# Reading the first block's queries in fp32 on a hardware queue, constants on the other queue, and a new instruction order, in a fused attention and feed-forward kernel

## The chip, the core and the metric

The kernel runs on one core of a Trainium2 chip. A core has TensorE (PE: matmuls and their weight loads), VectorE (DVE), ScalarE (ACT), GpSimd (POOL) and SyncE (SP), each with its own instruction stream that is worked off in order, and 16 DMA engines that all queues share. SP and ACT issue DMAs on hardware queues; GpSimd issues on the software queue, the only one here that converts fp32 to fp16 on the way. The metric is the device time of one execution in microseconds. A profile is of one execution; its span is the time from the first to the last instruction of the program.

## The reference

Attention over 4 batches, 8 heads, 768 positions and head size 64, with a sliding window of 128 and 4 sink positions that all see, and then a feed-forward layer on the 3072 tokens of 512.

```python
scores = scale * np.matmul(q, k.transpose(0, 1, 3, 2))
keep = is_sink | in_window              # j < 4, or 0 <= i - j < 128
a = softmax(np.where(keep, scores, -1e9))
x = np.matmul(a, v)                     # heads side by side: 3072 x 512
h = x @ w_in                            # 512 x 2048
g = h * (1.0 / (1.0 + np.exp(-1.702 * h)))
return g @ w_out                        # 2048 x 512
```

All inputs and the output are fp32. The kernel computes in fp16 with fp32 sums.

## The kernel before

**Tiling.** The sequence is cut into 24 blocks of 128 positions, 6 to a batch. A block holds all 8 heads. `ORDER` gives the places in which they are worked on: the first four places are blocks 0, 6, 12 and 18, the first of each batch, which need no block before them; then 1, 2, 3 and so on. Two neighbouring places make a pair, and the feed-forward layer runs over 12 pairs (`g`, numbered from 0) of 256 tokens.

**A block's steps.** Queries and keys (`qkn`) are transposed to `qkT`: on TensorE for the first eight places (`tq`, lines 398 and 405) with an eviction by VectorE or ScalarE (lines 355 and 359), by a DMA of SP for later pairs (line 433). Scores go to `own` and, for blocks with one before them, `prv` and `snk` (lines 481 and 510). For the first four places two matmuls per block write the causal mask into `own` ahead of the scores (`masks`, line 473). VectorE packs, takes the maximum (`mx`, line 537) and subtracts it (`e`, line 578); ScalarE takes the exponent (`a`, line 617). `a` is transposed to `at`, on TensorE for the first six places (`ta`) and by a DMA of SP for the rest (line 682). GpSimd cuts `at` into two triangles, `at` and `atp` (the selects, lines 620 and 624). TensorE multiplies with the values (`av`, lines 709 to 719), VectorE norms (`xn`, lines 726 and 727), and `xn` is transposed to `xT`, on TensorE for early blocks (`tx`) and by a DMA of SP from pair 3 on (line 758).

**Feed-forward.** For a pair, 8 groups of `hT` (line 780) are followed by the gate on ScalarE (line 810; for pair 0 a tanh on ScalarE and a multiplication on VectorE, lines 794 and 801), and 4 steps for each of two outputs `o` (line 834), an eviction to `osb` and a store. `w_in` and `w_out` are each loaded in four pieces (`i0` to `i3` and `o0` to `o3`; lines 293 and 302).

**Loads.** The software queue of GpSimd loads and converts `q`, `k` and `v` of nearly all blocks, one DMA each (lines 277 and 284; `v` at line 255, after VectorE has set the ones column of `v65`, line 232). Blocks of the first four places are read in rows of eight positions (`big`), so a packet has 2 KB of fp32; later ones and all of `v` have packets of one head's row of 64. One load is different: the keys of place 0, named in `CFG["hw"]`, are read in fp32 by SP to `raw_k` (line 263) and rounded by VectorE to `qkn` (line 271). The constants `consts` (identity, mask) are also read by SP (line 226). `vsb`, the sinks' values, is zeroed once (line 231).

**Order.** Every step is added to a planner with the engines that it may run on and estimated costs, and the order of all 834 steps, with the engine of each, is written out in the string `SEQUENCE`, which `Plan.run` reads: `12t` is step 12 on GpSimd, and p, a, d, s stand for PE, ACT, DVE, SP. The costs (`xfer`, `post` and the others) were used where the order was searched; at run time only `SEQUENCE` counts. Since each load is a step, an edit to the list `loads` renumbers the steps.

Of the kernel before, what the change touches and what calls it, by code (L numbers as in the profile page):

```python
# [36 lines left out]
    gbatch={},  # L37
    tanh=(0, 1),
    last=(256, 128, 128),
    hw=["k0"],  # L40
    big=(0, 1, 2, 3),
    avb={0: ("mi", "mm"), 1: ("mi", "mm"), 2: ("mi", "mm")},
    hb={},
    tqb={0: ("mm", "mi"), 1: ("mm", "mi")},
    actq=0,
    after0=25.0,
    vsb=15.0,
    slack={'v': 1, 's': 1, 'x': 1, 'e': 0.0, 'p': 0.0},
    steady=8,
    after=8.0,  # L50
    loads="q0 q1 k1 q2 k2 q3 k3 v0 v1 i0 i1 v2 v3 i2 i3 o0 o1 q4 k4 v4 o2 q5 k5 v5 o3".split(),
)
RING = dict(qkn=4, qkt=4, qk0=2, e32=4, a16=4, at=4, atp=4, xn=2, xt=4, gt=3, osb=4, mm=3, own=1, pv=1, mi=1, th=2)

SEQUENCE = """
0s 10d 4d 37s 12t 7d 14t 11a 16t 13t 106p 38d 15t 9d 2d 103p 6d 23t 3d 101p 104a 20t 126p 102a 18t 107p 127d 17t
124p 19t 108d 149p 109d 125a 22t 147p 150a 110d 129p 25t 148a 130p 111d 112a 105t 131d 113a 114p 132d 170p 115a 26t
116p 133d 171a 118p 152p 21t 117a 119d 153p 135a 134d 29t 120p 8d 137p 136a 121d 172p 33t 138a 154d 122p 173a 30t  # L60
139p 156d 123a 175p 155d 174t 140a 141p 481p 142d 158a 24t 157d 143p 176p 482a 144d 160p 34t 159a 483d 145p 161a 27t
177d 162p 484p 163a 146d 28t 179d 166p 487p 485a 167d 181a 486d 493p 488a 178d 489d 490p 40t 494a 180d 39t 478p 491a
495d 182a 32t 492d 183p 164p 479a 165d 499p 36t 184a 480d 185p 42t 500a 187p 195p 186d 193p 501d 48t 189p 196a 496p
190d 194a 168p 188d 497a 217p 215p 197p 169a 498d 218a 198p 191p 43t 199d 514p 192a 508p 216d 515a 200d 518p 46t
201d 509p 519a 31t 202d 239p 502p 240a 52t 203d 219p 128t 237p 221d 503p 238a 204a 520p 67t 222d 220p 510p 5d 223d
93s 504p 225d 224d 1s 242p 49t 94s 511p 151d 226a 45t 505p 512d 241p 521a 51t 506d 516p 243d 54t 524p 517a 244d 205p
525a 528p 206d 253p 245d 529a 255p 207t 522p 254d 247d 256a 246d 530p 35t 523a 227p 97t 208p 248a 228d 258p 257p
209d 270s 531p 259d 210t 230p 532p 260d 231a 229t 211p 261d 526p 249s 232t 212d 533p 527a 263d 262d 44t 233p 60t
536p 234d 264a 55t 213p 534d 537p 214d 41t 271p 538p 50t 273d 265s 235p 250t 539p 236a 274d 272p 548p 540a 296s 275d
550p 276d 57t 549a 552p 58t 277d 283p 53t 553a 544p 285d 551a 266t 554p 545a 286d 284p 251p 555a 287d 542p 61t 252d  # L70
546p 47t 288d 267p 56t 547a 556p 543a 268d 564p 289d 557a 269s 278a 558p 541s 297p 559p 299d 290a 565p 279s 300d
298p 566p 535s 301d 560p 96s 302d 291s 567p 303d 309p 304a 280t 95s 561p 311d 568a 305s 310p 578p 562d 570p 312d
579a 322s 292t 576p 98d 281p 571a 572p 66t 282d 584p 306t 313d 573a 507s 577a 513s 293p 585a 580p 294d 64t 574p 314d
581a 295s 84t 592p 575a 315d 316a 63t 307p 593p 59t 308d 586p 73t 317s 582p 72t 594p 99t 583a 587p 70t 323p 604p
325d 348s 595p 605a 326d 588p 596a 318t 324p 600p 327d 328d 589p 601a 598p 329d 65t 590d 335p 591s 78t 608p 563s
337d 62t 612p 609a 338d 69t 599a 336p 602p 613a 68t 339d 319p 603a 341d 340d 82t 606p 76t 620p 320d 607a 85t 342a
614p 100d 321s 79t 610p 361p 75t 330a 621p 343s 363d 91t 615p 611a 364d 331s 362p 616p 365d 622p 367d 366d 617p 623p
618a 632p 374s 624d 638p 636p 344t 639a 349p 637a 630p 351d 350p 626p 631a 352d 332t 345p 627a 634p 633a 346d 628p
353d 81t 640p 354d 629a 635a 333p 368a 648p 334d 642p 355d 347s 375p 356a 643p 569s 377d 641a 376p 357s 649p 378d
644p 369s 379d 650p 380d 645p 625s 656p 619s 646d 597s 381d 387p 358t 657a 400s 662p 389d 668p 663a 370t 651p 669a  # L80
359p 652a 388p 654p 360d 77t 658p 390d 74t 660p 659a 391d 80t 655a 371p 393d 392d 661a 71t 664p 372d 676p 665a 382a
373s 401p 670p 403d 647s 402p 671p 404d 394a 383s 666p 405d 677p 667a 406d 395s 672p 407d 413p 408a 673p 415d 384t
684p 674d 678p 416d 685a 409s 414p 679p 90t 417d 426s 692p 87t 680d 385p 418d 693a 396t 696p 419d 386d 686p 682p 88t
687a 397p 410t 683a 690p 697a 398d 688p 691a 399s 698p 689a 420a 694p 411p 699p 412d 695a 421s 700p 427p 675s 710p
429d 452s 712p 711a 430d 428p 701p 713a 422t 431d 720p 432d 724p 721a 702d 439p 725a 86t 433d 718p 441d 92t 716p
719a 442d 83t 440p 714p 717a 89t 423p 715a 732p 434a 424d 704p 443d 425s 445d 733p 444d 435s 722p 446a 705p 723a
681s 465p 447s 706p 467d 734p 703s 468d 466p 750p 436t 469d 735p 751a 470d 707p 736a 448t 742p 708a 746p 743a 437p
747a 738p 438d 748p 471d 739a 449p 749a 740p 472a 450d 744p 451s 453p 726p 745a 473s 455d 727p 456d 737s 454p 728p
741a 653s 457d 760p 459d 458d 752p 474t 729p 753a 460a 761p 730d 772p 762p 773a 461s 766p 763p 767a 780p 764a 770p
475p 462t 771a 768p 781a 476d 776p 769a 778p 777a 788p 779a 463p 774p 464d 782p 775a 477s 789p 765s 783p 731s 784p  # L90
790p 785p 796p 786d 791p 797a 754p 792a 808p 793s 709s 794p 787s 809a 802p 795a 755p 803a 806p 756p 807a 798p 800p
799a 757p 801a 804p 758d 822p 759s 805a 810p 816p 811p 823p 812p 824p 813p 817p 814a 825p 818p 826a 815s 828p 819p
827s 829p 820d 830p 831p 821s 832a 833a
"""


# [69 lines left out]
def kernel(  # L166
# [28 lines left out]
    plan = Plan(RING)  # L195
# [26 lines left out]
    def by(e):  # L222
        return nc.sync if e == SP else nc.scalar
# [19 lines left out]
    )  # L243

    def sw(key, cost, fn, xfer, **kw):
        return plan.add(POOL, key, cost, fn, xfer=xfer, post=0.9, **kw)

    ld, qkn = {}, {}

    def load_block(which, b, key, after=0.0):  # L250
        bb, r = divmod(b, 6)
        pair, i = divmod(PLACE[b], 2)
        src = {"q": q, "k": k, "v": v}[which][bb, :, r * P : (r + 1) * P, :].rearrange("h s d -> s h d")
        if which == "v":
            return sw(key, 0.88, lambda b=b, x=2: nc.gpsimd.dma_start(v65[:, b, :, 0:D], src), 0.88 if pair < 4 else 0.95, deps=[z_1], after=after)  # L255
        w = "qk".index(which)
        buf = qkn[pair]
        if which + str(PLACE[b]) in CFG["hw"]:
            raw = const.tile([P, H * D], FP32, name=f"raw_{which}{b}")
            n = CFG["hw"].index(which + str(PLACE[b]))  # L260
            src = {"q": q, "k": k}[which][bb, :, r * P : (r + 1) * P, :].rearrange("h (t e) d -> t h (e d)", e=8)
            got = plan.add(
                {SP: 0.45, ACT: 0.6}, -120 + n, 0, lambda e, src=src, raw=raw, x=9: by(e).dma_start(raw, src), xfer=0.75, post=0.6
            )

            def round16(e, b=b, w=w, i=i):
                dst, src = buf()[:, i, w].rearrange("p h d -> p (h d)"), raw
                if e == ACT:
                    nc.scalar.copy(out=dst, in_=src)
                else:  # L270
                    (nc.vector if e == DVE else nc.gpsimd).tensor_copy(out=dst, in_=src)

            return plan.add({DVE: 0.42, ACT: 0.6, POOL: 0.8}, -110 + n, 0, round16, deps=[got], take=[buf])
        if PLACE[b] in CFG["big"]:
            return sw(
                key, 0.64,
                lambda b=b, w=w, i=i: nc.gpsimd.dma_start(  # L277
                    buf()[:, i, w].rearrange("p h d -> p (h d)"),
                    {"q": q, "k": k}["qk"[w]][bb, :, r * P : (r + 1) * P, :].rearrange("h (t e) d -> t h (e d)", e=8),
                ),  # L280
                0.7, take=[buf], after=after,
            )
        return sw(
            key, 0.88, lambda b=b, w=w, i=i: nc.gpsimd.dma_start(buf()[:, i, w], src), 0.88 if pair < 4 else 0.95,  # L284
            take=[buf], after=after,
        )
# [4 lines left out]
    def load_w_in(f, key):  # L291
        def go(f=f, x=0):
            nc.gpsimd.dma_start(  # L293
                w_in16[:, :, bass.ts(f, 512)],
                moe_w_in.rearrange("(c p) f -> p c f", p=P)[:, :, bass.ts(f, 512)],
            )

        return sw(key, 0.8, go, 2.5)

    def load_w_out(f, key):  # L300
        def go(f=f, x=1):
            nc.gpsimd.dma_start(
                w_out16[:, bass.ts(f, 4)],
                moe_w_out[bass.ts(f, 512), :].rearrange("(c p) f -> p c f", p=P),
            )

        return sw(key, 0.8, go, 2.5)

    for n, what in enumerate(CFG["loads"]):
        w, x = what[0], int(what[1:])  # L310
# [584 lines left out]
```

## Time and profile before

| | before |
|---|---|
| times | 229.1, 229.35, 229.35 us; median 229.35 |
| profiled execution | 228.31 us, span 226.6 us |
| TensorE busy | 214.5 us (95%) |
| VectorE, ScalarE, GpSimd busy | 136.2, 136.6, 113.5 us |
| DMA moved | 32.47 MB, mean 143 GB/s |
| granted TensorE clock | 1.00 |

The page cuts the span into 40 slices of 5.7 us; each digit is the busy share in tenths:

```profile
PE   1889899999999999999899999999999999999994
DVE  0899898998896852796286677843957371111010
DMA  6999999999999999999998998999998072042112
```

TensorE starts after the first loads and is nearly always busy from the second slice to the last. The DMA engines are busy from the first slices on until three quarters of the span. A chain or a wait that names a DMA tells which load or transpose landed last before an instruction could start.

### The profile page before, as it was taken

What the parts mean: (1) busy time and instruction counts of PE and PEld (TensorE: products, weight loads), DVE (VectorE), ACT (ScalarE), POOL (GpSimd) and SP (SyncE); (2) the same over time, 40 slices, a digit from 0 to 9 for tenths busy, and PEclk for the clock granted to TensorE, in tenths of its full rate; (3) what the DMA queues carried; (4) which work ended last, traced back from release to release, by engine and by line L of the source; (5) the groups of instructions that cost most, each with busy time, mean ns of one, the idle gap of its engine ahead of it and who ended that gap; (6) DMA issues with size and microseconds to landing.
All of it is one profiled execution on the core that took longest, in us unless ns stands there. A gap on an engine that the chain in (4) does not pass through costs nothing.

```text
span 226.6 us, 5625 instructions
## 1 busy us (share of the span) xinstructions
PE 214.5 (95%) x2378; PEld 151.7 (67%) x2378; DVE 136.2 (60%) x243; ACT 136.6 (60%) x190; POOL 113.5 (50%) x135
## 2 busy tenths in 40 slices
PE   1889899999999999999899999999999999999994
PEld 0658876776784785675675685686765956856763
DVE  0899898998896852796286677843957371111010
ACT  2588696796746766367349249848585669613511
POOL 8955654698980689397071670780816112300000
PEclk9999999999999999999999999999999999999999
DMA  6999999999999999999998998999998072042112
GB/s 128 174 205 196 178 191 191 156 142 137 134 164 157 203 210 156 120 219 134 148 174 133 260 138 144 127 147 130 150 116 198 4 191 38 17 138 77 66 46 93
DMA packets 123512, 32.47 MB, mean 143 GB/s; under 512 B 114880, under 2 KB 120416, under 8 KB 123488
## 3 DMA queue, kind: packets, MB, share of 16 engines
q0 software_dynamic: 71792, 13.51, 79.6%
q1 hardware_dynamic: 51552, 18.55, 44.7%
q8 instruction: 18, 0.29, 0.6%
q10 hardware_dynamic: 144, 0.07, 0.1%
q14 instruction: 6, 0.05, 0.1%
HBM read 27.46 MB, written 6.29 MB: 149 GB/s over the span
## 4 chain that ended last, share of the span: by engine, by line
PE 77%; DMA 10%; POOL 5%; DVE 2%; ACT 1%; SPq 1%; issue 1%; POOLq 0%; DVEq 0%
PE o L834 33%; PE hT L780 31%; DMA w_in<-in_moe_w_in_dram 6%; DMA at<-a 4%; PE own L481 3%; PE av L715 2%; PE av L719 2%; PE av L709 2%; PE prv L481 2%; POOL qkn L277 2%; SPq L682 1%; POOL v L255 1%; POOL w_in L293 1%; PE tq L405 1%; PE snk L510 1%
## 5 line engine op out<-in xcount | busy, mean ns | idle before, releaser
L780 PE MATMUL hT<-xT,w_in 128*128 128x256 f16 (+1 forms) x896 | 94.1, 257 | 1.4 <-DMA xT<-xn 0.6
L834 PE MATMUL o<-w_out,gT 128*128 128x512 f16 (+2 forms) x416 | 91.8, 363 | 0.0
L810 ACT ACTIVATE gT<-hT 128x512 f16<-128x512 f32 x88 | 50.9, 597 | 58.7 <-PE hT L780 58.4
L780 PEld LDWEIGHTS <-w_in 128*128 128x128 f16 x896 | 75.3, 98 | 14.5 <-DMA xT<-xn 1.1
L834 PEld LDWEIGHTS <-gT 128*128 128x128 f16 x416 | 37.2, 98 | 32.2
L620 POOL TENSOR_SCALAR_AFFINE_SELECT atp<-at 128x1024 f16<-128x1024 f16 (+1 forms) x22 | 22.2, 1009 | 65.7 <-DMA at<-a 64.7
L527 DVE COPY_PREDICATED own<-consts,prv 128x1024 f32<-128x1024 uint16 x20 | 24.6, 1229 | 24.3 <-PE prv L481 24.2
L537 DVE TENSOR_REDUCE mx<-own 128x8 f32<-128x1024 f32 (+1 forms) x28 | 29.7, 1068 | 0.9 <-PE own L481 0.4
L578 DVE TENSOR_TENSOR e<-own,mx 128x1024 f32<-128x1024 f32 (+1 forms) x28 | 29.8, 1066 | 0.9
L617 ACT ACTIVATE a<-e 128x1056 f16<-128x1056 f32 (+1 forms) x28 | 26.2, 952 | 4.9 <-issue 2.6
L624 POOL TENSOR_SCALAR_AFFINE_SELECT at<-at 128x1024 f16<-128x1024 f16 (+1 forms) x22 | 22.5, 1024 | 1.5
L355 DVE COPY osb<-o 128x512 f32<-128x512 f32 (+1 forms) x12 | 8.0, 666 | 24.3 <-PE o L834 24.3
L284 POOL DMA_DIRECT2D qkn<-in_k_dram x20 | 17.8, 902 | 7.4 <-DMA w_out<-in_moe_w_out_dram 5.1
L255 POOL DMA_DIRECT2D v<-in_v_dram x24 | 21.4, 902 | 0.0
L726 DVE RECIPROCAL rcp<-av 128x8 f32<-128x8 f32 (+1 forms) x28 | 5.5, 195 | 26.5 <-PE av L719 26.4
L284 POOL DMA_DIRECT2D qkn<-in_q_dram x20 | 17.8, 894 | 2.3 <-DMA qkn<-in_k_dram 0.7
L810 ACT ACT_TABLE_LOAD x14 | 18.0, 1283 | 0.2
L727 DVE TENSOR_TENSOR xn<-av,rcp 128x512 f16<-128x512 f32 (+1 forms) x28 | 17.2, 615 | 1.0
L715 PE MATMUL av<-v,at 128*128 128x65 f16 x192 | 17.0, 194 | 0.6 <-POOL at L624 0.5
L617 ACT ACT_TABLE_LOAD x13 | 16.7, 1283 | 0.2
L715 PEld LDWEIGHTS <-at 128*128 128x128 f16 x192 | 14.2, 98 | 2.5 <-POOL at L624 1.2
L481 PEld LDWEIGHTS <-qkT 64*128 64x128 f16 x352 | 10.2, 96 | 7.8 <-issue 5.1
(56 smaller groups left out, 165.9 us busy)
## 6 DMA issues: line engine op xcount, KB each, us to landing
out_dram<-osb SPq DMA_DIRECT2D x23, 256.0 KB, 2.5
qkn<-in_q_dram POOLq DMA_DIRECT2D x24, 128.0 KB, 5.3
v<-in_v_dram POOLq DMA_DIRECT2D x24, 128.0 KB, 5.6
qkn<-in_k_dram POOLq DMA_DIRECT2D x23, 128.0 KB, 8.6
w_in<-in_moe_w_in_dram POOLq DMA_DIRECT2D x4, 512.0 KB, 10.2
w_out<-in_moe_w_out_dram POOLq DMA_DIRECT2D x4, 512.0 KB, 11.6
at<-a SPq DMA_TRANSPOSE x18, 3.3
raw_k<-in_k_dram SPq DMA_DIRECT2D x1, 256.0 KB, 4.6
```

What stands on the lines that cost most here:

```text
L255: return sw(key, 0.88, lambda b=b, x=2: nc.gpsimd.dma_start(v65[:, b, :, 0:D], src), 0.88 if pair < 4 else 0.95, deps=[z_1], after=after)
L284: key, 0.88, lambda b=b, w=w, i=i: nc.gpsimd.dma_start(buf()[:, i, w], src), 0.88 if pair < 4 else 0.95,
L527: nc.vector.copy_predicated(out=own(lo, hi).rearrange("p l j s -> p (l j) s"), mask=later.unsqueeze(1).to_broadcast((P, 4 * (hi - lo), P)) ...
L537: lambda lo=lo, hi=hi, own=half, small=small: nc.vector.tensor_reduce(out=small[:, lo:hi], in_=own(lo, hi), axis=AX.X, op=ALU.max),
L578: nc.vector.tensor_tensor(out=e32()[:, 512 * lo : 512 * hi].rearrange("p (l j s) -> p l j s", j=4, s=P), in0=own(lo, hi), in1=small[:, lo: ...
L617: nc.scalar.activation(out=a16()[:, lo:hi], in_=e32()[:, lo:hi], func=AF.Exp, scale=scale)
L620: nc.gpsimd.affine_select(out=atp()[:, lo : lo + n], in_=at()[:, lo : lo + n], pattern=[[0, n], [-1, P]], compare_op=ALU.is_gt, fill=0.0, ...
L624: nc.gpsimd.affine_select(out=at()[:, lo : lo + n], in_=at()[:, lo : lo + n], pattern=[[0, n], [1, P]], compare_op=ALU.is_ge, fill=0.0, ba ...
L715: nc.tensor.matmul(acc[:, j], at()[:, c], v65[:, b, h], start=(r == 0), stop=(r == 0))
L780: nc.tensor.matmul(ht()[:, n], w_in16[:, c, bass.ts(f, P)], xt[g]()[:, tok, c], start=(c == 0), stop=(c == 3))
L810: lambda fs=fs, cols=cols, gt=gt, ht=ht: nc.scalar.activation(out=gt()[:, fs[0] : fs[-1] + 1, cols], in_=ht(), func=AF.Gelu_apprx_sigmoid),
L834: nc.tensor.matmul(po(), gt()[:, F, bass.ts(t, P)], w_out16[:, F, cols], start=(F == 0), stop=(F == NF - 1))
```

## The change

The queries of place 0 join its keys in `CFG["hw"]`: both are read in fp32 by SP, keys first, and rounded by VectorE. The constants may now be issued by SP or ACT, and the new order has them on ACT, ahead of its first table load. `q0` leaves the list of software loads. Some estimated costs are edited, and `SEQUENCE` is another one throughout.

```diff
-    hw=["k0"],
+    hw=['k0', 'q0'],
...
-    actq=0,
+    actq=1,
...
-    loads="q0 q1 k1 q2 k2 q3 k3 v0 v1 i0 i1 v2 v3 i2 i3 o0 o1 q4 k4 v4 o2 q5 k5 v5 o3".split(),
+    loads="q1 k1 q2 k2 q3 k3 v0 v1 i0 i1 v2 v3 i2 i3 o0 o1 q4 k4 v4 o2 q5 k5 v5 o3".split(),
...
-0s 10d 4d 37s 12t 7d 14t 11a 16t 13t 106p 38d 15t 9d 2d 103p 6d 23t 3d 101p 104a 20t 126p 102a 18t 107p 127d 17t
+0a 38s 8d 36s 2d 10d 4d 7d 18t 11a 12t 13t 39d 17t 104p 16t 37d 105a 19t 102p 15t 107p 103d 14t 6d 108p 21t 125p 24t
...
-        return plan.add(POOL, key, cost, fn, xfer=xfer, post=0.9, **kw)
+        return plan.add(POOL, key, cost, fn, xfer=xfer, **{"post": 1.1, **kw})
...
-                {SP: 0.45, ACT: 0.6}, -120 + n, 0, lambda e, src=src, raw=raw, x=9: by(e).dma_start(raw, src), xfer=0.75, post=0.6
+                {SP: 0.45, ACT: 0.6}, -120 + n, 0, lambda e, src=src, raw=raw, x=9: by(e).dma_start(raw, src), xfer=0.9, post=0.6
...
-                key, 0.64,
+                key, 0.56,
...
-        return sw(key, 0.8, go, 2.5)
+        return sw(key, 0.8, go, 2.5, post=2.0)
```

What the new order does with the steps that the prediction speaks of, by the instruction order of both programs:

| | before | after |
|---|---|---|
| SP, first | consts, raw_k | raw_k, raw_q |
| GpSimd, first loads (by block) | q0 k6 k12 q6 q12 v12 v6 k18 q18 v0, then i1 i2 | v0 q6 k6 k18 q18 v6 k12 q12, then i1 i2 i3 |
| then | sink keys, i3 i0 q1 q2 k1, sink keys, v18 k2 o0 o1 k3 q3 o2 o3 | sink keys, i0 v12 q2 k1 q1, zeroing of vsb, v18 k2 k3 o0, sink keys, q3 o1 o2 o3 |
| TensorE, first | masks, tq of block 0's keys and queries, tq of block 6's keys, scores of block 0 | tq of block 0's keys and queries, masks, scores of block 0, tq of block 6 |
| GpSimd, loads between the selects of places 11 and 13 (counted from 0) | v13 q19 v11 q15 v14 k20 k17 k21 k19 q17 k23 | v19 v11 |
| zeroing of vsb | VectorE | GpSimd |
| eviction of block 18's queries and of block 0's first `ta` | ScalarE | VectorE |
| eviction of `xT` of block 6 | VectorE | ScalarE |

More of the change, by code (lines that the diff above doesn't have):

```diff
@@ L57 @@
 SEQUENCE = """
-0s 10d 4d 37s 12t 7d 14t 11a 16t 13t 106p 38d 15t 9d 2d 103p 6d 23t 3d 101p 104a 20t 126p 102a 18t 107p 127d 17t
[L59 to L92, printed above, removed]
@@ L93 @@
-827s 829p 820d 830p 831p 821s 832a 833a
+0a 38s 8d 36s 2d 10d 4d 7d 18t 11a 12t 13t 39d 17t 104p 16t 37d 105a 19t 102p 15t 107p 103d 14t 6d 108p 21t 125p 24t
+109d 127p 126a 111d 25t 128a 110d 113a 171p 129t 112d 130p 115p 9d 20t 131p 114a 172d 150p 132d 22t 151a 148p 116d
+32t 134d 117p 149a 119p 133d 118a 153p 29t 136a 135d 121p 154p 28t 120d 173p 137a 138p 122d 174a 3t 156d 139a 123p
+140p 124a 155d 176p 142p 141a 157d 482p 23t 158d 144p 483a 485p 33t 145d 159a 143d 177p 486a 484d 161p 487d 162a
@@ new lines @@
+146p 160a 179d 488p 41t 147a 178d 163p 489a 181d 494p 164a 180d 495a 490d 491p 26t 182a 496d 106t 167p 165p 492a
+479p 168d 183a 40t 493d 184p 480a 166d 500p 27t 185a 481d 31t 186p 501a 188p 194p 187d 196p 35t 502d 190p 195a 497p
+191d 197a 61t 169p 189d 498a 218p 44t 216p 198p 170a 499d 219a 43t 192p 200d 515p 217a 193a 519p 201d 516a 50t 199p
+503p 202d 42t 204d 520a 203d 509p 240p 221p 220p 241d 30t 238p 222d 510p 239a 205a 504p 223d 521p 46t 224d 511p 226d
+5d 225d 94s 243p 505p 1s 227a 242p 49t 512p 522a 47t 506p 513d 34t 244d 517p 507a 175t 529p 245d 518a 64t 254p 530a
@@ new lines @@
+256p 246d 525p 52t 255a 248d 531p 257d 45t 526a 247d 206p 228p 207a 98t 259p 532p 229d 249a 271s 208t 209p 258p 210d
+231p 260d 533p 211t 523p 261d 230t 212p 524a 250s 232d 534p 262d 233t 213d 527p 263d 53t 234p 528a 537p 55t 264d
+235d 265a 538p 56t 535d 236p 70t 272p 539p 58t 274d 237a 266s 214p 251t 273p 540p 215a 275d 549p 541a 276d 297s 553p
+277d 550a 57t 543p 62t 278d 284p 51t 554a 547p 286d 48t 551p 548a 287d 267t 252p 552a 545p 544a 253d 285p 555p 546a
+288d 59t 268p 289d 556a 557p 279a 269d 559p 290d 270s 298p 565p 291a 300d 280s 560p 558a 301d 566p 95s 299p 567p
@@ new lines @@
+514s 302d 542s 304d 579p 303d 96s 568p 292s 580a 281t 305a 310p 571p 323s 312d 561p 152d 569a 311p 282p 313d 572a
+306s 293t 581p 314d 562p 283d 582a 577p 563d 54t 508s 99d 583p 67t 316d 315d 573p 584a 68t 294p 100d 574a 307t 575p
+578a 295d 593p 576a 296s 317a 585p 73t 308p 74t 587p 309d 65t 586a 318s 594p 69t 595p 60t 324p 596p 77t 326d 325p
+71t 605p 597a 327d 599p 606a 328d 588p 319t 600a 329d 613p 349s 336p 614a 81t 603p 338d 63t 607p 604a 330d 339d 320p
+608a 601p 321d 589p 602a 322s 611p 570s 609p 612a 536s 337p 598s 590p 610a 340d 331a 342d 621p 341d 615p 362p 343a
@@ new lines @@
+616p 364d 622p 344s 365d 617p 332s 591d 363p 623p 366d 618p 367d 629p 619a 345t 350p 620s 630a 564s 624p 352d 97s
+637p 333t 375s 368d 353d 346p 638a 639p 625a 347d 351p 76t 627p 640a 354d 90t 334p 355d 628a 631p 79t 356d 335d 641p
+82t 632a 348s 635p 80t 642a 633p 66t 636a 376p 72t 634a 643p 369a 378d 78t 649p 379d 644p 357a 377p 650p 380d 382d
+645p 381d 358s 659p 383a 370s 646p 660a 651p 647d 401s 388p 669p 390d 359t 389p 663p 670a 391d 652p 648s 664a 392d
+661p 85t 393d 655p 371t 662a 653d 360p 656a 394d 654s 665p 361d 592s 384s 657p 372p 658a 667p 666a 373d 395a 671p
@@ new lines @@
+374s 402p 672p 404d 385t 668a 396s 677p 405d 403p 673p 406d 83t 697p 407d 86t 678p 698a 408d 414p 75t 409a 674p 416d
+93t 685p 397t 417d 679p 686a 410s 675d 386p 101d 683p 427s 387d 415p 680p 684a 691p 681d 398p 692a 411t 689p 399d
+695p 418d 690a 400s 687p 419d 92t 696a 412p 89t 688a 420d 693p 413d 88t 699p 694a 84t 421a 428p 91t 700p 430d 717p
+431d 725p 422s 718a 429p 701p 432d 434d 702p 433d 453s 713p 703d 440p 714a 719p 442d 423t 441p 721p 720a 443d 726a
+715p 722a 87t 444d 711p 446d 445d 424p 712a 705p 716a 425d 435a 723p 426s 466p 733p 704s 468d 447a 436s 706p 469d
@@ new lines @@
+724a 734p 448s 467p 735p 470d 472d 626s 707p 682s 749p 437t 736p 750a 708p 737a 449t 753p 709a 743p 754a 739p 744a
+438p 740a 747p 439d 745p 471d 450p 746a 751p 748a 451d 727p 452s 741p 676s 454p 742a 728p 752a 456d 473a 455p 729p
+457d 761p 458d 730p 459d 474s 762p 460d 773p 731d 461a 763p 774a 462s 779p 475t 764p 732s 780a 710s 767p 765d 769p
+768a 463t 476p 770a 775p 477d 781p 771p 782a 776a 464p 772a 755p 465d 777p 478s 756p 778a 766s 789p 757p 790p 758p
+795p 759a 791p 796a 783p 797p 792p 798a 784p 793a 809p 794s 738s 785p 810a 799p 786p 800a 801p 787d 807p 788s 802a
@@ L94 @@
+803p 808a 805p 804a 823p 806a 811p 824p 812p 825p 813p 814p 817p 815a 818p 826p 816s 819p 827d 760s 820p 828s 829p
+821d 830p 831p 822s 832p 833a 834a
 """
@@ L305, in go @@
             )
-        return sw(key, 0.8, go, 2.5)
+        return sw(key, 0.8, go, 2.5, post=2.0)
     for n, what in enumerate(CFG["loads"]):
```

## Prediction

> **What bounds the kernel now.** I read the page first, then TensorE's waits, then the timeline of the first 14 us, then the table by stretches of time, and last the DMA issues with their landings.
>
> ```profile
> span 226.6 us, 5625 instructions
> PE 214.5 (95%) x2378; PEld 151.7 (67%) x2378; DVE 136.2 (60%) x243; ACT 136.6 (60%) x190; POOL 113.5 (50%) x135
> ```
>
> TensorE is busy for 214.5 of 226.6 us. The matmuls of the changed program are the same ones, so only the 12.1 us of idle time can move: 8.9 us before the last matmul ends at 223.5, and a tail of 3.1. TensorE's waits say where the 8.9 lies:
>
> ```profile
> PE own L473 <- DMA consts<-cconst: 2.9, 1, 2.9
> PE tq L398 <- DVE qkn L271: 2.4, 1, 2.4
> PE hT L780 <- DMA xT<-xn: 0.6, 1, 0.6
> PE hT L780 <- DMA w_in<-in_moe_w_in_dram: 0.6, 1, 0.6
> PE tx L745 <- DVE xn L727: 0.5, 2, 0.3
> PE av L715 <- POOL at L624: 0.5, 1, 0.5
> ```
>
> The first two are the start (5.26 us). Sorted by time, the gaps from 7.36 to 25.8 us add 2.27, and those from 60 to 119 us add 1.38 (0.15 at 60.9, 0.63 at 109.0, 0.53 at 115.1, 0.07 at 119.1). Between and after these TensorE never stops. The start in the timeline:
>
> ```profile
> 0.81 0.35 SPq L226 DMA_DIRECT2D consts<-cconst  x1
> 1.22 0.75 SPq L263 DMA_DIRECT2D raw_k<-in_k_dram  x1
> 1.32 0.68 POOL L277 DMA_DIRECT2D qkn<-in_q_dram  x1 [0.80 <-POOLq L876]
> 2.86 1.03 PE L473 MATMUL own<-consts 128*128 128x512 bf16 x2 [2.86 <-DMA consts<-cconst]
> 5.81 0.43 DVE L271 CAST qkn<-raw_k 128x512 f16<-128x512 f32 x1 [3.94 <-DMA raw_k<-in_k_dram]
> 6.29 1.07 PE L398 MATMUL tq<-consts,qkn 128*64 128x64 f16 x32 [2.40 <-DVE qkn L271]
> 8.18 0.61 PE L481 MATMUL own<-qkT 64*128 64x128 f16 x8
> 8.28 0.69 DVE L355 CAST qkT<-tq 128x512 f16<-128x512 f32 x1 [0.73 <-PE tq L398]
> 8.89 1.28 DVE L537 TENSOR_REDUCE mx<-own 128x4 f32<-128x512 f32 x2
> ```
>
> The mask matmuls (L473) fill dead time. What ends the wait at 6.29 is the keys (raw_k lands at 5.79), not the queries (q0's landing is 5.55). So moving q0 alone removes no wait; what can help is that raw_k stands first on its queue. The stretches after that:
>
> ```profile
> 12.00:18.00 6.00, 5.18 (x94) 3.67 (x92) 5.86 (x15) 5.31 (x11) 3.29 (x7) 1.00 1.25 207
> 18.00:24.00 6.00, 4.94 (x87) 4.30 (x84) 5.91 (x13) 4.45 (x8) 2.41 (x4) 1.00 1.69 185
> ```
>
> The columns are TensorE, weight loads, VectorE, ScalarE, GpSimd, clock, DMA share, GB/s. VectorE has 11.77 of 12 us here; TensorE has slack. The DMA engines are as full: the fourth w_in piece is issued at 10.41 and lands at 23.41, k/q/v of later blocks are issued only as older ones land, and w_out's pieces land at 30.02, 32.63, 36.80 and 39.40, each less than about 1.5 us before its first matmul.
>
> **The change, part by part.** The costs edited in the planner (post, xfer, cost) time nothing by themselves, since SEQUENCE is written out.
>
> *Consts to ScalarE's queue.* SP's first issue is now raw_k, at 0.81 instead of 1.22. ScalarE issues before its table load: 0.37 us (row of its one DMA of before), so the warm-up ends near 2.7 instead of 2.3; its first real work was at 6.97, so this is hidden, up to 4 us.
>
> *raw_k.* Issue to first packet took 0.96 us for consts (0.81 to 1.77 in the trace's packets) and 2.14 for raw_k (1.22 to 3.36). Its 128 packets of 2 KB take 96 ns each, 0.77 us over 16 engines alone; beside q0 they took 1.86 (3.36 to 5.22); landing followed 0.57 later. So it now lands between 0.81+0.96+0.77+0.57 = 3.1 and 0.81+2.14+1.86+0.57 = 5.4. I take raw_k's own delay of 2.14, and 1.1 for the packets, because its neighbour is now v0, whose packets are 32 ns: 4.6.
>
> *raw_q.* It follows on the same queue with the same packets: 0.8 to 1.1 later, 3.9 to 6.3; I take 5.5. The software-queue q0 cost the same (98 ns a packet), so DMA time neither rises nor falls, and GpSimd saves one issue of 0.68. Its cast on VectorE is one more of 0.43.
>
> *The first block.* Keys: cast to 5.1, 16 matmuls (half of the 1.07) to 5.65. Queries: cast 5.5 to 5.95, matmuls to 6.5. The masks now stand behind these, 1.03, to 7.53; beside them VectorE moves the queries out (0.69, to 7.3). Scores start at 7.55, not 8.18: 0.63 earlier. But before had also done block 1's keys by then (16 matmuls, 0.50), so TensorE is ahead by 0.13 only. In general the scores start at raw_q's landing + 2.0, and TensorE's idle time until then is raw_q's landing minus 0.1, against 5.5 before; the two meet at 5.6.
>
> *VectorE after that.* By the order of instructions it gains two evictions (block 3's queries 0.69, a first at 0.42) after the first maximum and loses xT of block 6 (0.42); the zeroing of vsb (0.93) and block 1's keys were before it. So 0.69 more work from a start 0.63 earlier: level. Where VectorE is the limit (12 to 24 us) the lead is used up; from 24 to 30 it has 0.9 idle. I charge 0.4, bounds 0 and 0.7.
>
> *vsb's zeroing on GpSimd.* No row has it; between the 0.93 on VectorE and twice that. It stands ahead of v18, k2, k3 and w_out. GpSimd waited 2.1 and 1.5 us for w_in landings there, so it is hidden; without that cover 0.9 to 1.9 us.
>
> *Loads.* Two v loads, not three, stand ahead of w_in (v took 1.3 between landings), and all four w_in pieces come so much earlier. The 0.56 gap at 22.89 (the w_in wait and its edge) goes: -0.56, bounds -0.56 and 0.
>
> Early sum: -0.13 + 0.4 - 0.56 = -0.3.
>
> *The middle.* The waits at 109 and 115 us come from transposes that crawl behind loads: an xT issued at 101.22 landed at 109.62, an at issued at 106.71 at 116.75, against medians of 5.3 and 3.3.
>
> ```profile
> at<-a SPq DMA_TRANSPOSE x18, 3.3
> xT<-xn SPq DMA_TRANSPOSE x9, 5.3
> ```
>
> There GpSimd issued eleven loads in a row, from 96.8 to 106.5, between the selects of the 12th and 14th place in ORDER. In the new order two stand there, the others before and behind. So 0.63 + 0.53 + 0.07 = 1.23 goes. New tight places: TensorE work between a pair's last av and its first hT, summed from the rows (0.87 per 8 hT, 0.86 per 4 o, 0.55 for own and prv), is 5.0 us for pair 7 (was 8.1) and 5.8 for pair 3 (was 9.1). What must fit in is a norm (0.8), 0.1, and an xT landing of 3.04 (issued 200.14) to 5.65 (issued 67.83): 3.9 to 6.6. So pair 7 waits 0 to 1.6 and pair 3 0 to 0.8; with few loads near the first and a drained burst near the second I take 0.4 and 0.3. The av of the 19th place has 14.3 us behind its scores (was 16.9): 0.1. Middle sum: -1.23 + 0.8 = -0.43, bounds -1.2 and +1.3.
>
> The tail gets one more output of 256 KB on SP ahead of the last pieces; SP issues took 0.4 there with over a second free between, so nothing, at most 0.4.
>
> Sum: 228.31 (226.6 span, 1.71 around) - 0.3 - 0.43 = 227.6. The profiled execution is 1.04 under the median, so I forecast 229.35 - 0.75 = **228.6**. About 0.2% (0.46 us) is what a measurement can tell from no change.
>
> **Rivals.**
> *Issue time only.* All queues feed engines that are full from 3.5 us on; raw_k gets its 0.41 of earlier issue, less the 0.5 of undone work, and the middle trades waits one for one: 229.3, chance 0.14. For it: first slice at 6 tenths of DMA, all others at 9. Against: the eleven loads did move. [...]
>
> *Queries late.* One queue now carries both; if raw_q lands after 5.6 us, TensorE starts later in all. With raw_k at 5.4 and 1.1 more it is 6.5: idle 6.4 against 5.5, so +0.9, and with the middle unchanged 230.3. For it: raw_k needed 4.6 us to land, and q0 had 4.2 on the other queue. Against: nothing is ahead of raw_k any more. Chance 0.15.
>
> *Pair 7 waits on its xT.* From a landing of 4.1 us it costs. At the median of 5.3 it is 1.2, with pair 3's 0.8 +2.0, against the 1.23 saved and no early gain: 230.1. Against: the new order puts one load (q21) between 108 and 127 us of TensorE work. Chance 0.15.
>
> **How the numbers follow.** The forecast has 0.56, the rivals 0.14, 0.15 and 0.15; the forecast's bounds (early -1.1, middle -1.2) reach 227.3, the two slow rivals 230.3, cut at 230.2. Faster 0.56, same 0.14, slower 0.30.
>
> **What would show it.** Right: raw_k landing by 4.6 and raw_q by 5.5, scores of block 0 near 7.5, no w_in wait on TensorE, no waits at 105 to 120 us. Wrong: queries cast after 6 us; a TensorE wait on xT near 75 or 140 us; VectorE still full to 24 us with gaps on TensorE before 30 us as large as before (2.3 us).

## Result and profile after

The changed kernel takes 240.27 us (median of four runs, 238.75 to 241.61) against 229.35 us. The ratio is 1.0497, interval 1.0458 to 1.0536: 5% slower. The forecast was 228.6 us, the range ended at 230.2. The ratios here are estimated from undisturbed executions alone, so they differ a little from a quotient of the medians (1.048 here), which take in slow ones too.

The profiled execution took 241.61 us, 13.3 us more than the one of before (228.31). The medians differ by 10.9, because the profiled execution of before lies 1.04 under its median and this one 1.34 over. The sums below are made against the 13.3. The page after:

```profile
span 239.9 us, 5627 instructions
PE 217.3 (91%) x2378; PEld 153.6 (64%) x2378; DVE 137.5 (57%) x243; ACT 137.0 (57%) x191; POOL 112.8 (47%) x134
PE   1888899972999699997999899999999999999994
PEclk9999999996799999999999999999999999999999
```

A slice is 6.0 us here. TensorE falls to 7 and 2 tenths in slices 9 and 10 (counted from 1, about 48 to 60 us), and its granted clock falls to 6 and 7 tenths just behind. The difference splits so: TensorE's idle time ahead of its last matmul goes from 8.9 to 19.5 us (+10.6), its busy time from 214.5 to 217.3 (+2.8), and the tail stays at 3.1. Of the idle time, 8.53 us lies before 30 us (was 7.56) and 10.97 behind (was 1.38). So some 9.6 of 13.3 us are new waits in the middle. TensorE's waits name them (in total, times, longest):

```profile
PE tq L398 <- DVE qkn L271: 5.9, 2, 5.2
PE av L709 <- POOL vsb L334: 4.5, 1, 4.5
PE av L715 <- POOL at L624: 2.7, 3, 1.4
PE own L481 <- DMA qkT<-qkn: 2.2, 1, 2.2
PE hT L780 <- DMA xT<-xn: 1.0, 1, 1.0
PE hT L780 <- DMA w_in<-in_moe_w_in_dram: 0.6, 1, 0.6
```

The first line is the start. By the time at which they begin, the large ones behind it are 4.51 at 52.73 (ahead of the first `av` that reads `vsb`, for place 4), 0.92 at 57.61 and 0.45 at 59.37 (`av` behind selects), 2.20 at 78.66 (scores of place 10 behind the transposed queries and keys of pair 5), 1.37 at 108.68 (`av` of place 11) and 1.04 at 137.18 (`hT` of pair 7 behind its `xT`): 10.5 together. The largest is a wait for GpSimd, so the next view is GpSimd's own timeline:

```profile
44.91 0.87 POOL L284 DMA_DIRECT2D qkn<-in_q_dram  x1
54.20 0.87 POOL L284 DMA_DIRECT2D qkn<-in_q_dram  x1 [8.41 <-DMA qkT<-qkn]
55.06 0.88 POOL L255 DMA_DIRECT2D v<-in_v_dram  x1
56.07 1.11 POOL L334 TENSOR_TENSOR vsb<-vsa,ownm 32x520 f16<-32x520 f32 x1
57.15 0.62 POOL L620 TENSOR_SCALAR_AFFINE_SELECT atp<-at 128x512 f16<-128x512 f16 x1
57.85 0.63 POOL L624 TENSOR_SCALAR_AFFINE_SELECT at<-at 128x512 f16<-128x512 f16 x1
```

GpSimd stands still for 8.41 us in front of a load, and behind this load in its order are a v load, `vsb` of the first batch and the selects of places 4 and 5. Before, `vsb` was written at 47.38; here at 56.07. The load is of the queries of block 8 (pair 5), step `52t` (q8). What releases it is a transpose into `qkT`: SP's queue has

```profile
49.14 1.90 SPq L433 DMA_TRANSPOSE qkT<-qkn  x1
```

which is the one of pair 4, and it landed at 53.63. So q8's place in `qkn` is the buffer that pair 4 is still read from; the built program has both pairs at the same address. `qkn` is a ring of four (`RING["qkn"]`), a buffer for each of four pairs at a time; the load at 44.91, the queries of block 13 (step `64t`, q13, pair 7), which nobody needs until much later, had been given the buffer that pair 2 left. (The first load of pair 6, q11, stands early too, ahead of pair 4's, and holds the buffer of pair 0.)

The start, from the same view of all engines:

```profile
4.62 0.48 DVE L271 CAST qkn<-raw_k 128x512 f16<-128x512 f32 x1 [2.62 <-DMA raw_k<-in_k_dram]
5.15 0.64 PE L398 MATMUL tq<-consts,qkn 128*64 128x64 f16 x16 [5.15 <-DVE qkn L271]
5.70 0.81 DVE L271 CAST qkn<-raw_q 128x512 f16<-128x512 f32 x1 [0.61 <-DMA raw_q<-in_q_dram]
7.13 1.03 PE L473 MATMUL own<-consts 128*128 128x512 bf16 x2
8.10 0.61 PE L481 MATMUL own<-qkT 64*128 64x128 f16 x8
```

The scores of block 0 start at 8.10 (8.18 before): the keys' cast comes 1.2 us earlier, but the masks, which filled dead time before, now stand in front of the scores.

### The profile page after: what moved, and what is told of

It reads as the page before. It is cut to its first block, busy times and chain, and to the rows that moved or that the text cites. A ratio compares the mean times of both kernels' runs of the same rounds, so it can differ in the third digit from the quotient of the medians.

```text
span 239.9 us, 5627 instructions
## 1 busy us (share of the span) xinstructions
PE 217.3 (91%) x2378; PEld 153.6 (64%) x2378; DVE 137.5 (57%) x243; ACT 137.0 (57%) x191; POOL 112.8 (47%) x134
## 4 chain that ended last, share of the span: by engine, by line
PE 60%; DMA 27%; POOL 7%; DVE 2%; issue 1%; ACT 1%; SPq 0%; POOLq 0%; DVEq 0%
PE o L834 27%; PE hT L780 24%; DMA qkT<-qkn 6%; DMA qkn<-in_q_dram 5%; DMA qkn<-in_k_dram 5%; DMA v<-in_v_dram 5%; DMA xT<-xn 3%; PE own L481 2%; POOL qkn L284 2%; PE av L715 2%; DMA raw_q<-in_q_dram 2%; PE av L719 2%; POOL at L624 2%; POOL atp L620 1%; PE av L709 1%; PE prv L481 1%
## 5 line engine op out<-in xcount | busy, mean ns | idle before, releaser
L780 PE MATMUL hT<-xT,w_in 128*128 128x256 f16 (+1 forms) x896 | 95.1, 258 | 2.0 <-DMA xT<-xn 1.0
L834 PE MATMUL o<-w_out,gT 128*128 128x512 f16 (+2 forms) x416 | 93.0, 365 | 0.2 <-ACT gT L810 0.2
L780 PEld LDWEIGHTS <-w_in 128*128 128x128 f16 x896 | 76.1, 98 | 17.2 <-DMA xT<-xn 1.5
L355 DVE COPY osb<-o 128x512 f32<-128x512 f32 (+2 forms) x13 | 8.3, 636 | 30.1 <-PE o L834 26.3
## 6 DMA issues: line engine op xcount, KB each, us to landing
w_in<-in_moe_w_in_dram POOLq DMA_DIRECT2D x4, 512.0 KB, 10.5
```

Source lines behind the costliest of these rows:

```text
L780: nc.tensor.matmul(ht()[:, n], w_in16[:, c, bass.ts(f, P)], xt[g]()[:, tok, c], start=(c == 0), stop=(c == 3))
L834: nc.tensor.matmul(po(), gt()[:, F, bass.ts(t, P)], w_out16[:, F, cols], start=(F == 0), stop=(F == NF - 1))
```

## Experiments

The theory: the loss comes from GpSimd standing in front of q8 for a buffer, with `vsb` and the selects queued behind, and its consequences; the new start is harmless. The rivals: the new start is at fault (a hardware queue that carries both block 0 loads, a later software queue), or the half clock, or the whole new order with many small losses. In the diffs, only the moved words of `SEQUENCE` are shown.

**Start and order taken apart (e3, e4).** e3 is the old order with the new start: the steps renumbered, constants on ACT, raw_k then raw_q on SP, no q0 on GpSimd. e4 is the opposite: the new order with constants and raw_k on SP and q0 on GpSimd.

```diff
 # e3, against the kernel before; SEQUENCE renumbered
-    hw=["k0"],  actq=0,  loads="q0 q1 ...
-0s 10d 4d 37s 12t 7d ...
+    hw=['k0', 'q0'],  actq=1,  loads="q1 ...
+0a 10d 4d 38s 36s 7d ... 39d 37d ...
 # e4, against the changed kernel; SEQUENCE renumbered
-    hw=['k0', 'q0'],  actq=1,  loads="q1 ...
+    hw=["k0"],  actq=0,  loads="q0 q1 ...
-0a 38s 8d 36s 2d 10d 4d 7d 18t ...
+0s 37s 8d 12t 2d 10d 4d 7d 19t ...
```

Expected of e3: 

> The old order with the new start alone: raw_k and raw_q first on SP, consts on ScalarE's queue, q0 no more on GpSimd; all other steps stand as before. Theory (GpSimd blocked; the start is nearly level): 228.5 to 230.5, with TensorE's first matmuls (the masks) at 2.8 as before, raw_k landing at 4.6 and raw_q at 5.7. Rival 1 (new start costs): above 234. My predicted first block gives scores about 0.6 us earlier and a gain of 0 to 1 us.

Expected of e4: 

> The new order with the old start: consts and raw_k on SP, q0 by the software queue ahead of v0, everything else in the new order, with q8 ahead of the selects. Theory (GpSimd blocked): the 8.4 us wait and the half clock are here as well; 238 to 242. Rival 1 (new start): 229 to 232. Rival 2 (DMA backlog): 238 to 242 as well, so this run tells only the start apart.

e3 took 228.62 us, ratio 0.996 (0.9932 to 0.9988): slightly faster than the kernel before, and the lowest ratio of all (f3, below, is level with it). e4 took 238.3 us, ratio 1.0423 (1.0364 to 1.0481), and its waits have the same pattern as the changed kernel's:

```profile
PE av L708 <- POOL vsb L333: 3.9, 1, 3.9
POOL qkn L283 <- DMA qkT<-qkn: 8.5, 1, 8.5
```

(Lines of kernels with a rewritten order are one lower.) The loss is in the order, not in the start: the intervals of e4 and of the changed kernel overlap, although e4's keys landed at 7.10 us and its first matmul came at 7.61 (4.59 and 5.15 in the changed kernel).

**q8 itself moved (e1).** q8 goes behind the second select of place 5; it still waits for the same buffer, but nothing near is behind it.

```diff
-256p 246d 525p 52t 255a
+256p 246d 525p 255a
 ...
-233t
+233t 52t
```

Expected: 

> The changed kernel with one step moved in GpSimd's order: the load of block 8's queries (q8) stands behind the four selects of places 4 and 5, not ahead of v4, vsb0 and those selects. Theory (GpSimd blocked): q8's buffer is the one of pair 4, so its load waits 8.4 us for that pair's transposing DMA, and TensorE then waits 4.5 + 0.9 + 0.45 us for what is queued behind it and loses 2.8 us more at half clock. Then the wait on vsb and the half clock go, and the time is 240.3 - 8.6 = 231.7, give or take 1.5. Rival 1 (the new start is what costs): stays above 238. Rival 2 (DMA backlog; whatever is first on GpSimd would be late): another wait of 2 to 5 us takes its place between 50 and 60 us, 234 to 239.

Measured: 235.24 us, ratio 1.0241 (1.019 to 1.0291). The GpSimd wait and the `vsb` wait are gone, and so is half of the loss. The expected size (231.7, give or take 1.5) was missed, and the time lies where rival 2 had it (234 to 239). But no new wait stands between 50 and 60 us, as that rival needs: the new ones are 2.04 at 68.70 for a select and 0.98 at 74.80 for `qkT`. The four loads of pair 5 and two far ones are issued only from 54.9 to 60.2 us, with the selects done. In the profiled execution TensorE's idle time ahead of its last matmul is 13.3 us (19.5 in the changed kernel), so 6.2 went, and the busy time stays high, 217.7: full clock comes first at 15.99 us (14.68 in the changed kernel, 11.73 in the one before), and the clock is half again for 3.41 us from 70.61 on, where the gap of 2.04 ends. The waits for selects and for `qkT`:

```profile
PE av L714 <- POOL at L623: 2.7, 2, 2.0
PE own L480 <- DMA qkT<-qkn: 1.0, 1, 1.0
```

**A fifth buffer (e2).** The order untouched, q8 need not wait.

```diff
-RING = dict(qkn=4,
+RING = dict(qkn=5,
```

Expected: 

> The changed kernel with five buffers for qkn instead of four; the order is untouched. Pair 5 then gets the buffer of pair 2, long free. Theory (GpSimd blocked by the buffer): no 8.4 us wait on GpSimd, no wait on vsb, no half clock; 231 to 232. Rival 1 (new start): above 238. Rival 2 (DMA backlog): q8 issues early but vsb0 and the selects still come late because the DMAs are; 234 to 239.

Measured: 232.70 us, ratio 1.0158 (1.011 to 1.0205). This is 0.7 over what the theory expected and below both rivals: q8 is early, and `vsb` (46.55 us) and the selects are not late, so a backlog of DMAs is not what held them up. There is no wait of GpSimd on `qkT`, none of TensorE on `vsb`, full clock from 11.07 us to the end, and TensorE is busy for 214.5 us as before. What is left in its waits:

```profile
PE tq L398 <- DVE qkn L271: 5.9, 2, 5.1
PE av L715 <- POOL at L624: 2.6, 2, 1.8
PE own L481 <- DMA qkT<-qkn: 2.2, 1, 2.2
```

**The far load moved instead (g1).** Ring of four, q8 where it was; only q13 goes behind k10 (step `59t`), a load of pair 6.

```diff
-518a 64t 254p
+518a 254p
 ...
-59t
+59t 64t
```

Expected: 

> The changed kernel with four buffers, and one step moved: the first load of pair 7 (q13, needed some 45 us of TensorE work later) stands behind k10 instead of ahead of q8. q8 itself stays where it was, ahead of v4, vsb0 and the selects. Theory (the early far load takes the free buffer, that of pair 2, and pair 5 is left with pair 4's): q8 no longer waits, no 8.4 us wait on GpSimd, no wait on vsb, no half clock; 231 to 233, as with five buffers. Rival (q8 is too early in any case): the wait stays, 238 or more.

Measured: ratio 1.0109 (1.0038 to 1.0181), 231.95 us on a chip where the kernel before took 228.45. In the built program pair 5 now has pair 2's buffer. GpSimd's timeline shows q8 in its old place without a wait and `vsb` at 45.86:

```profile
43.52 0.88 POOL L283 DMA_DIRECT2D qkn<-in_q_dram  x1
44.39 0.88 POOL L254 DMA_DIRECT2D v<-in_v_dram  x1
45.86 1.12 POOL L333 TENSOR_TENSOR vsb<-vsa,ownm 32x520 f16<-32x520 f32 x1 [0.59 <-DVE e L601]
```

The place of this one word of 835 holds about four fifths of the loss (1.0497 to 1.0109; by g1's interval 64 to 92%). With e2 it shows the cause of this part: a load that was not urgent took the free buffer ahead of one that was.

**What is left with five buffers: loads and masks (f1, f2, g4).** f1 is e2 with the near loads k8 and q9 right behind q8 and the far q13 and q15 (pairs 7 and 8) behind k10. f2 is e2 with the first masks ahead of the first scores' transposes. g4 has both.

```diff
 # f1, against e2
-64t ... 53t ... 55t ... 70t          (q13, k8, q9, q15 where they stood)
+52t 53t 55t ... 59t 64t 70t
 # f2, against e2
-104p ... 107p
+107p 104p
```

Expected of f1: 

> Five buffers for qkn, and four loads moved on GpSimd: k8 and q9 of pair 5 to right behind q8, ahead of v4, vsb0 and the selects, and q13 and q15 of pair 7 to behind k10. What is left over the old order (232.7 against 228.6) is put down by theory L (order of loads) to k8, q9 and k9 landing late, so that pair 5's transposing DMA lands at 73.2 and not 67.8 and TensorE waits 2.2 us for it: then that wait goes and the time is 230.5, give or take 0.8. Rival M (masks and other early work): the middle wait is replaced by another and the time stays at 232 to 233.

Expected of f2: 

> Five buffers for qkn, and the first block's mask matmuls (1.03 us) stand first on TensorE, as in the old order, instead of behind both transposes. Theory L (order of loads): the first idle time falls by about 1 us of 5.9 and the end by 0.3 to 1.0 (VectorE limits from 12 to 24 us): 231.7 to 232.4. Rival M: the missing masks and the later start of TensorE's activity are most of what the new order lost, 229.5 to 231.

Expected of g4: 

> The new order with five buffers and both repairs: the four loads moved (k8, q9 forward, q13, q15 back) and the first masks ahead of the transposes. Theory: the two gains (1.7 and 0.9 us against five buffers alone) add up nearly: 229.8 to 230.6, still above the old order with the new start. Rival (they overlap, both only filled the same slack): 231.

f1: 230.99 us, ratio 1.0061 (1.0028 to 1.0094), as expected; the wait of `own` on `qkT` fell from 2.2 to 0.4:

```profile
PE av L714 <- POOL at L623: 1.3, 1, 1.3
PE own L480 <- DMA qkT<-qkn: 0.4, 1, 0.4
```

f2: 231.76 us, 1.0081 (1.005 to 1.0113). g4: 230.34 us, 1.0082 (1.0044 to 1.0121). Against e2 (1.0158) each repair is worth 0.8 to 1% alone, and the two together no more than one. g4's time is in the expected span, but on a chip where the kernel before is 1.1 us faster than on that of f1 and f2 (228.45 against 229.59); by the ratios the two do not add. One reason shows in the waits: f2 moves no load, and yet its wait on `qkT` is 0.6 and those on selects add 0.5, where e2 has 2.2 and 2.6. So what f1 was to remove is nearly gone in f2 too, and that the place of the loads makes e2's 2.2 is not shown. The remaining 0.8% of g4 over the kernel before stays open.

**Is the fifth buffer itself a gain? (f3)** e3 with `qkn=5`.

Expected: 

> The old order with the new start and five buffers for qkn. Theory (in the old order no load is held up for long by a buffer; GpSimd waits 0.6 us for a transpose of pair 4): 228 to 228.7, no difference of over 0.3% from the old order with the new start. Rival (buffers hold loads up all along): 226 to 227.5.

Measured: 228.83 us, 0.9967 (0.9947 to 0.9987), as e3's 0.996. In the old order a fifth buffer does nothing that can be measured, so e2's gain is the removal of a wait that the new order made.

**The half clock (f4).** The changed kernel with 20 matmuls of 128x512 into a free bank, whose result nobody reads, in the gap ahead of place 4's `av`.

```diff
+for _ in range(20 if b == 1 else 0):
+    nc.tensor.matmul(bank(lo), ident, w_in16[:, 0, 0:512], start=True, stop=True)
```

Expected: 

> The changed kernel with 20 more matmuls of 128x512 in front of the av of place 4 (some 4.3 us at full clock), into the bank that av then overwrites; they need nothing that is late, so they fill the 4.5 us gap. Theory (the half clock follows from the idle TensorE): GpSimd's wait is the same, the granted clock stays 1.0 and the time falls by about 2.8 to 237.5. Rival (the half clock is not tied to the gap, or its cost lies under other waits): 240 or more.

Measured: 241.81 us, ratio 1.0541 (1.0487 to 1.0595); no gain, where one was expected. The clock did stay full: from 12.58 us past the last matmul in the profiled execution, and 0.993 to 1.000 on average in f4's four runs (0.984 to 0.986 in those of the changed kernel). The same stretch, 56 to 62 us, of the changed kernel and then of f4 (columns: length, TensorE, weight loads, VectorE, ScalarE, GpSimd, granted clock, DMA share, GB/s):

```profile
56.00:62.00 6.00, 3.39 (x23) 1.59 (x23) 1.48 (x3) 0.00 (x0) 5.65 (x9) 0.50 0.67 44
```

```profile
56.00:62.00 6.00, 4.13 (x59) 2.71 (x58) 2.21 (x5) 0.89 (x2) 5.73 (x10) 1.00 0.41 30
```

So the half clock goes with the idle gap. GpSimd's wait stayed (8.8 us). The last matmul ended at 235.41 instead of 236.85, 1.4 us earlier, but the tail grew from 3.06 to 4.55: the last three stores of SP took 4.2 to 4.5 us to land, not 2.0 to 2.3. That the half clock costs something on the total isn't shown.

**The start in the old order (g2, g3).** g2 moves only the constants to ACT, in the kernel before. g3 is e3 with five idle-time matmuls at the start, two ahead of the transposes of block 0's keys and three ahead of those of its queries.

```diff
 # g2, against the kernel before
-    actq=0,        0s 10d 4d ...
+    actq=1,        0a 10d 4d ...
 # g3, against e3
+for _ in range((3, 2)[w] if p == 0 else 0):
+    nc.tensor.matmul(dst, identb, bias0.unsqueeze(1).to_broadcast((P, 4, P)), start=True, stop=True)
```

Expected of g2: 

> The old order with one part of the new start: consts on ScalarE's queue, so raw_k is SP's first DMA; q0 stays on the software queue. Theory (raw_k's place alone is what helps; q0's queue changes no wait): the time is that of the old order with the whole new start, 0.996 of before, 228.2 to 229.0; raw_k lands near 4.8. Rival (both parts are needed): 229.3 to 229.8, as before.

Expected of g3: 

> The old order with the new start, and five more matmuls of 128x512 in the idle time of TensorE between 3.9 and 6.7 us (two ahead of the transposes of block 0's keys, three ahead of its queries', into the banks that these overwrite). Theory G (TensorE's small matmuls run slow until it has been busy for some time, at 10.0 to 14.7 us in the runs so far; activity from 2.9 us on opens this earlier, by about 7 us or soon after): the slow rows end 3 us earlier and the time falls by 0.3 to 0.8 to 227.8 to 228.3. Rival V (VectorE and the DMAs set the pace up to 25 us, so it gains nothing): 228.4 to 229.0, no change against the old order with the new start.

g2: 229.14 us, 1.002 (0.9983 to 1.0056), no difference. So the theory, 0.996 by raw_k's place alone, missed and the rival's "as before" holds, though raw_k landed at 4.38 instead of 5.79 and the scores of block 0 started a whole microsecond earlier:

```profile
5.30 1.07 PE L397 MATMUL tq<-consts,qkn 128*64 128x64 f16 x32 [1.24 <-DVE qkn L270]
7.18 0.61 PE L480 MATMUL own<-qkT 64*128 64x128 f16 x8
```

The lead is lost early: TensorE's idle time ahead of 30 us is 7.78 us, against 7.56 before. The two gaps of the start are 1.0 us shorter together (4.26 instead of 5.26), and new ones of 0.46 at 10.09, 0.66 at 10.95 (for a load of queries) and 0.47 at 20.31 take their place.

g3: 229.41 us, 1.0037 (1.0002 to 1.0071); the filling buys nothing and is behind e3, even outside what rival V expected. Full clock came at 8.34 us instead of e3's 10.05, 1.7 us earlier and not 3, so the "about 7 us" of theory G was an estimate that g3 does not bear out. The profiled execution is g3's slowest and has a wait of 2.26 us at 120.89 for a `qkT`, and half clock behind it. How e3's gain of 0.4% splits between raw_k's place and the queries on SP stays open: the intervals of g2 and e3 touch. e3's own start shows what they bring together:

```profile
2.90 1.03 PE L472 MATMUL own<-consts 128*128 128x512 bf16 x2 [2.90 <-DMA consts<-cconst]
4.38 0.43 DVE L270 CAST qkn<-raw_k 128x512 f16<-128x512 f32 x1 [2.50 <-DMA raw_k<-in_k_dram]
6.23 0.43 DVE L270 CAST qkn<-raw_q 128x512 f16<-128x512 f32 x1 [1.43 <-DMA raw_q<-in_q_dram]
8.04 0.61 PE L480 MATMUL own<-qkT 64*128 64x128 f16 x8 [0.25 <-ACT qkT L358]
```

Here the masks are done in dead time at 2.90, and the scores start at 8.04, although the queries land 0.5 us later than in the changed kernel.

## Why the prediction was wrong

**The step that failed** is the pricing of GpSimd's loads. The prediction compared where loads stand between the selects of places 11 and 13, and called GpSimd's other waits covered. It did not ask, of the loads that the new order moved earlier, whether their destination is free at that point, and what compute stands behind them on GpSimd, so its sum has no term for this: it was put at nothing without a reason. The runs showed 8.41 us in front of q8, and 5.9 us of TensorE waits for `vsb` and the selects behind it. The place of q13 ahead of q8, and of q8 ahead of `vsb` and the selects of places 4 and 5, is in the instruction order of the changed program, and the built program lists pair 4's transpose among the things that q8's load waits for: this could be read without a run. The middle sum had bounds of -1.2 and +1.3; the idle time there rose by 9.6. No rival had this mechanism either: their waits came from a DMA that lands late, never from an engine that stands in front of a full ring. A hint was in the trace of before, whose GpSimd waited 0.6 us on a `qkT` transpose in front of q11; there the selects were already done.

**Point by point.**

- raw_k by 4.6, raw_q by 5.5: landed at 4.59 and 5.68. Right within 0.2, for raw_k with some luck: its first packet came 1.51 us after the issue, not 2.14, and from there to the landing it took 2.27, not 1.67. raw_q is past the 5.6 at which the prediction saw no more gain; TensorE's idle time until the scores is 5.9 us (5.5 before), so the rival "queries late" had its condition by a little, and cost 0.4.
- Scores of block 0 at 7.55: 8.10. raw_q is 0.18 late, its cast took 0.81 instead of 0.43, the group of 16 matmuls 0.64 instead of 0.53; the masks behind them took the forecast 1.03. A cast from fp32 took 0.76 in e2, 0.85 in g2 and 0.43 in e3, and why is not known.
- The zeroing of `vsb` on GpSimd, taken as 0.93 to 1.9 us and hidden, took 0.96, and GpSimd waited for `w_in` behind it (1.19, 1.67 and 2.86 us): hidden, as forecast.
- The w_in gap gone (-0.56): it stayed, 0.58 at 23.56. The term assumed that the software queue starts as early as before. Its first load is now v0, which waits for VectorE's ones column and is issued at 2.25 instead of 1.32. The first w_in piece landed at 15.24 (15.40 before), the fourth at 24.09 (23.41). v0's place alone does not set this: e2, with the same order, has the fourth piece at 22.91 and a wait of 0.2 us for it.
- Early sum -0.3: ahead of 30 us the idle time rose by 0.97. With the old order behind it (e3), the new start gives -0.4% of 229.5, or -0.9 us (-1.6 to -0.3 by the interval). That is no test of this sum, which was made for the new order's start.
- No waits at 105 to 120 us for places 12 and 13: they are gone, as forecast. But place 11 has one of 1.37 at 108.68: its `at` was issued at 99.12, amid seven loads that GpSimd issued from 96.6 to 102.8, and landed at 107.62, 8.5 us later against a median of 3.5. The crawl behind a burst of loads met another place.
- Pair 7 waits on its `xT`: 1.04, within the 0 to 1.6 that the middle sum gave it, taken as 0.4. The `xT` itself took 8.2 us to land, not 3.0 to 5.7: GpSimd issued eight loads from 126.2 to 133.2 us around it, where the prediction saw few. Pair 3 had no wait of note.
- The 2.20 for pair 5's `qkT` was not foreseen. The pair's transpose was issued at 70.22 and landed at 80.81. It does not hang on q8's wait: e2, where q8 does not wait, has 2.22, and e4, where it waits 8.5, has no such wait. In every run of the new order that transpose took 9.2 to 11.1 us to land, against 8.3 in the kernel before; what of this becomes a wait differs from run to run and was not settled.
- The rise of busy time by 2.8 goes with the half clock; the prediction took the busy time as fixed. The clock record has half clock for 6.83 us from 55.64 us on, and full clock first at 14.68 us, against 11.73 before. e2, with full clock from 11.07 us on and no later gap in it, is busy for 214.5 us, as before.
- The range's lower end, 227.3, does not follow from its terms. No part gives an early bound of -1.1 (they give -0.13 + 0 - 0.56 = -0.7), and -1.1 and -1.2 from 229.35 make 227.05. It had no part in the miss.

Of 5.0%, the far load's claim on the free buffer makes up 3.4 (e2) to 3.9 (g1). That the rest is order too is argued from e3, where the start alone costs nothing: of the 1.6% that e2 leaves, f1 and f2 each take about half, and 0.8% (g4) stays open.

## What to carry to other kernels

When an order is changed, list every load on a compute engine's queue whose buffer is not free yet, and read which work of that engine stands behind it: here the load that waited for its buffer held up GpSimd for 8.41 us, with `vsb` and the selects behind it. The free buffer of the ring went to the load that came first in the order (q13, not q8), so put loads in the order in which they are needed, and hold a far load back until the near ones have theirs (1.0497 to 1.0109 in g1). One more buffer showed in a single run that the ring was at fault (1.0497 to 1.0158 in e2); in the old order it made no difference (0.9967 in f3 against 0.996 in e3).

## What the runs showed of the hardware

**The clock and gaps.** The clock records of the profiled executions begin with full clock, first between 8.34 (g3) and 15.99 us (e1). In the kernel before it came at 11.73 us, and two mask matmuls took 1.03 us at 10.14 and 0.59 at 12.88. Behind that and ahead of the last matmul, the half clock came in lengths of 3.41 or 6.83 us: 6.83 in the changed kernel after a gap of 4.51, 6.83 in e4 after 3.86, 3.41 in e1 after 2.04, 3.41 in g3 after 2.26. It did not come after gaps of 2.20 (changed kernel, 78.66) or 2.22 (e2). So the length of a gap alone, between 2.04 and 2.26 us, did not decide it here; what did is not shown.

**Transposes behind loads.** In the changed kernel, DMA transposes that were issued among many software-queue loads took 8.5 us (`at`, 99.12 to 107.62), 8.2 (`xT`, 129.97 to 138.18) and 10.6 (`qkT`, 70.22 to 80.81, with nine loads issued from 62.3 to 72.5), against medians of 3.5, 3.0 and 4.5 in the same execution.

**What an earlier start is worth.** In g2 the scores of block 0 started 1.00 us earlier with the order otherwise unchanged, and the time did not change within its interval. In e4 TensorE's first matmul came 2.46 us later than in the changed kernel, and the time was not longer. The prediction's way of carrying a lead at the start to the end needs a check at each later point where a DMA or GpSimd sets the pace.
